# Attention read followed by a SiLU layer: the first w_in chunk in four transfers of 32 partitions, and three small early reads left out

## The chip, the cores and the metric

The kernel runs on one core of a Trainium2 chip. The core has five engines that run side by side, each with its own instruction queue: TensorE (PE, with its weight loads shown as PEld), VectorE (DVE), ScalarE (ACT), GpSimd (POOL) and SyncE (SP), which here only issues transfers. Transfers are carried out by 16 DMA engines that all queues share. The metric is the device time of one execution in microseconds (us), the median of several runs.

## The reference, cut to what matters

There are 8 batches of 8 heads, 512 positions of 64 numbers, and per head a state of 32 rows. Each position reads the state by attention, each state row reads the positions, and all 4352 rows, as vectors of 512, go through a layer with SiLU.

```python
scores = scale * np.matmul(x, state.transpose(0, 1, 3, 2))
a = softmax(scores)
xread = np.matmul(a, state)
scores2 = scale * np.matmul(state, x.transpose(0, 1, 3, 2))
sread = np.matmul(softmax(scores2), x)
x = concatenate([xread, sread], axis=2)   # then heads beside each other: 4352 x 512
h = x @ w_in                              # 512 x 2048
out = (h * (1.0 / (1.0 + np.exp(-h)))) @ w_out   # 2048 x 512
```

## The kernel before, in words

For the 512 position rows of a batch the kernel does not compute xread and multiply it by `w_in`; it computes W1 = state times `w_in` per batch (`w1_m`, L275, and `w1f_m`, L290, for the first chunk of batch 0), and then W1 times the transposed attention weights `aT` (`g1`, L313). W1 has four chunks of 512 columns. `g1(b, ft)` makes one of 16 blocks of 128 hidden columns, with SiLU on ScalarE into `g`; `g2` (L339) multiplies `g` by `w_out`. The sread rows of all batches go through `w_in` itself at the end (b = 8).

The order of every engine's instructions is written out by hand (`tc.manual_schedule`, L372): each engine runs its own in the order in which the Python code issues them, and waits on semaphores where data is not there. From L583 on a plan in steps of one `g2` matmul places the work of batches 2 to 7; before that, batch 0 and 1 are written out line by line.

What happens at the start:

- ScalarE's queue issues `st_f[0]` (L374, state of batch 0) and two of the three `tch` transfers (L375, L376); GpSimd issues the third (L383). A `tch` transfer reads 8 bytes from each eighth row of 128, 16 rows in four blocks, of `w_in` (columns 0 and 512) or `w_out`. Nothing uses what it brings.
- SP issues, in this order, the four quarters of x of batch 0 into `x_f` (L378, 256 KB each), `st_f[1]` (L379), the first 512 columns of `w_in` into `w_f` (L381, four transfers, one for each block of 128 rows of `w_in`, each over all 128 partitions) and the first quarter of `w_out` into `wo_f` (L437, four transfers). A DMA takes the next of eight semaphores in turn for the two hardware queues, so an issue can wait for the landing of the eighth one before it.
- TensorE runs filler matmuls on zeros (`warm`, L365) between the transposes of x (`x_T`, L140), the scores (`sc`, L172) and the transposes of state; VectorE and GpSimd cast x to bf16, ScalarE takes the exponential, VectorE and GpSimd normalise into `an` (L201, L213).
- After six fillers TensorE runs `w1f_m` (L478): W1 chunk 0 of batch 0 in float32 from `w_f` and `sbd_f`, eight matmuls of 64 rows by 32 columns of the array, for four blocks kt of `w_in` rows and two halves of 64 partitions; half 0 goes to bank w0 and half 1 to bank w1. The transposes of `an` (`a_T`, L223, matmuls at L229) stand behind them, then `g1(0, 0)` and `g1(0, 1)`.
- VectorE copies `aT`, a quarter of W1, casts `w_f` to bf16 into `w_in_sb` (L494 and L500, two blocks kt each; the copies themselves are recorded at L83), normalises sread (L257, L258) and casts `st_f[1]` (L496), whose transpose (L123) TensorE needs ahead of the first `g2`. GpSimd issues the loads of the other chunks (L101, L106) and of x of batch 1 (L95), and casts `wo_f` into `w_out_sb` (L475; recorded at L85).

Of the kernel before, what the change touches and what calls it, by code (L numbers as in the profile page):

```python
# [8 lines left out]
FP32 = mybir.dt.float32  # L9
# [10 lines left out]
def kernel(  # L20
# [8 lines left out]
    nc = tc.nc  # L29
    ds = bass.ds  # L30

    B, H, S, NS, D, DM, DF = 8, 8, 512, 32, 64, 512, 2048
    KT = 4
    SCALE = 0.125

    pers = ctx.enter_context(tc.tile_pool(name="pers", bufs=1))
# [3 lines left out]

    zeros = pers.tile([128, 512], BF16, name="zeros")
    ident = pers.tile([128, 128], BF16, name="ident")
    tch = [pers.tile([16, KT, 2], FP32, name=f"tch{i}") for i in range(3)]
    st_f = [pers.tile([128, 128], FP32, name=f"st_f{i}") for i in range(2)]
    w_f = pers.tile([128, KT, 512], FP32, name="w_f")
    wo_f = pers.tile([128, 4, DM], FP32, name="wo_f")
# [28 lines left out]
    win_re = moe_w_in.rearrange("(kt p) f -> p kt f", p=128)  # L75
    wout_re = moe_w_out.rearrange("(ft p) m -> p ft m", p=128)
# [211 lines left out]


    def w1f_m(bks):  # L290
        for kt in range(KT):
            for half in range(2):
                nc.tensor.matmul(  # L293
                    bank[bks[half]][ds(32 * kt, 32), :],
                    sbd_f[ds(64 * half, 64), kt, :],
                    w_f[ds(64 * half, 64), kt, :],
                    start=True,
                    stop=True,
                    skip_group_check=True,
                    tile_position=(64 * half, 32 * kt),  # L300
                )
# [70 lines left out]
    with tc.manual_schedule():  # L372

        nc.scalar.dma_start(st_f[0][:], state[0].rearrange("h ns d -> ns h d"))  # L374
        nc.scalar.dma_start(tch[0][:], win_re[0:128:8, :, 0:2])  # L375
        nc.scalar.dma_start(tch[1][:], wout_re[0:128:8, 0:4, 0:2])  # L376
        for kt in range(KT):
            load_x(0, nc.sync, kt, 1)  # L378
        nc.sync.dma_start(st_f[1][:], state[1].rearrange("h ns d -> ns h d"))  # L379
        for kt in range(KT):  # L380
            nc.sync.dma_start(w_f[:, kt, :], win_re[:, kt, 0:512])  # L381
        make_identity(nc, ident[:])
        nc.gpsimd.dma_start(tch[2][:], win_re[0:128:8, :, 512:514])  # L383
        nc.vector.memset(zeros[:], 0.0)
        nc.vector.memset(sbd[:], 0.0)
        for i in range(2):
# [89 lines left out]
        nc.scalar.preload_act_table(SILU)  # L476
        warm(6, "o0", 512)
        w1f_m(("w0", "w1"))  # L478
        w1_e(0, 0, ("w0", "w1"), ("act", "act"), 0, 256)
        a_T(0, (("a0", "dve"), ("a1", "dve")))  # L480
# [215 lines left out]
```

## Time and profile before

| what | value |
|---|---|
| median of 5 runs | 219.13 us (218.56 to 219.88) |
| the profiled execution | 219.13 us, its span 217.4 us |
| granted TensorE clock | 1.00 |
| DMA to landing, `x_f` by SP, 256 KB each | 3.9 us median |
| DMA to landing, `w_f` by SP, 256 KB each | 4.5 us median |
| DMA to landing, `wo_f` by SP, 256 KB each | 6.0 us median |
| DMA to landing, `tch`, 0.5 KB each | 3.6 to 3.7 us |

How to read the profile: its span runs from the first to the last instruction; the execution's own time is 1.7 us longer. L12 is line 12 of the kernel. A group of instructions is shown as line, engine, operation, output<-input and count, with the idle time of the engine ahead of it in brackets and what ended that. The chain that ended last is followed back from the last instruction: at each step to what released it, or to the instruction before it on its engine. Windows give, for a stretch of time, each engine's busy time and number of instructions, the clock, the mean busy share of the DMA engines (over 1 where an engine has several packets under way), and the GB/s written by them.

### The profile page before, as it was taken

What the parts mean: (1) busy time and instruction counts of PE and PEld (TensorE: products, weight loads), DVE (VectorE), ACT (ScalarE), POOL (GpSimd) and SP (SyncE); (2) the same over time, 40 slices, a digit from 0 to 9 for tenths busy, and PEclk for the clock granted to TensorE, in tenths of its full rate; (3) what the DMA queues carried; (4) which work ended last, traced back from release to release, by engine and by line L of the source; (5) the groups of instructions that cost most, each with busy time, mean ns of one, the idle gap of its engine ahead of it and who ended that gap; (6) DMA issues with size and microseconds to landing.
All of it is one profiled execution on the core that took longest, in us unless ns stands there. A gap on an engine that the chain in (4) does not pass through costs nothing.

```text
span 217.4 us, 4108 instructions
## 1 busy us (share of the span) xinstructions
PE 210.9 (97%) x1664; PEld 104.4 (48%) x1664; DVE 84.5 (39%) x176; ACT 134.3 (62%) x225; POOL 45.7 (21%) x87
## 2 busy tenths in 40 slices
PE   7989999999999999999999999999999999999993
PEld 7533454454444444444444444444454444566553
DVE  3775537832930463147313830275017401111110
ACT  3753485679767947884788458855885586233211
POOL 4696209300700070016001600070001000000000
PEclk9999999999999999999999999999999999999999
DMA  5999995695395149316831694146012311111112
GB/s 176 315 262 267 236 274 71 54 270 203 72 208 178 51 112 247 128 48 100 216 121 50 105 213 169 51 120 149 24 48 44 105 48 48 51 48 48 48 51 97
DMA packets 37555, 27.86 MB, mean 128 GB/s; under 512 B 22176, under 2 KB 31776, under 8 KB 37536
## 3 DMA queue, kind: packets, MB, share of 16 engines
q1 hardware_dynamic: 31280, 21.63, 37.3%
q0 software_dynamic: 5392, 5.44, 12.8%
q10 hardware_dynamic: 864, 0.53, 0.8%
q8 instruction: 13, 0.21, 0.4%
q14 instruction: 6, 0.05, 0.1%
HBM read 17.30 MB, written 8.91 MB: 121 GB/s over the span
## 4 chain that ended last, share of the span: by engine, by line
PE 94%; DVE 3%; ACT 1%; issue 0%; DVEq 0%; ACTq 0%
PE ps_o L342 28%; PE ps_w L342 26%; PE ps_h L318 25%; PE ps_h L329 3%; PE ps_o L367 2%; PE ps_a L175 2%; PE ps_a L278 1%; PE ps_w L293 1%; DVE w_in_sb L83 1%; PE ps_o L278 1%; PE ps_w L278 1%; PE ps_h L278 1%; DVE W L83 1%; PE ps_o L245 1%; DVE xT L83 1%; PE ps_a L143 0%
## 5 line engine op out<-in xcount | busy, mean ns | idle before, releaser
L326 ACT ACTIVATE g<-ps_h 128x512 bf16<-128x512 f32 x128 | 76.0, 597 | 36.4 <-PE ps_h L318 29.7
L318 PE MATMUL ps_h<-aT,W 128*128 128x512 bf16 x256 | 75.8, 379 | 0.2 <-DVE W L83 0.2
L342 PEld LDWEIGHTS <-g 128*128 128x128 bf16 x512 | 49.0, 98 | 54.9 <-issue 2.5
L342 PE MATMUL ps_w<-w_out_sb,g 128*128 128x512 bf16 x256 | 73.3, 379 | 0.0
L342 PE MATMUL ps_o<-w_out_sb,g 128*128 128x512 bf16 x256 | 65.9, 379 | 0.2
L318 PEld LDWEIGHTS <-W 128*128 128x128 bf16 x256 | 24.1, 98 | 27.8 <-DVE W L83 1.6
L201 POOL TENSOR_TENSOR an<-en,rs 128x512 bf16<-128x512 bf16 x8 | 8.4, 1054 | 111.9 <-ACT en L186 72.7
L83 DVE COPY o_sb<-ps_w 128x512 f32<-128x512 f32 (+1 forms) x13 | 8.5, 659 | 53.1 <-PE ps_w L342 53.0
L83 DVE COPY o_sb<-ps_o 128x512 f32<-128x512 f32 x14 | 9.5, 687 | 29.6 <-PE ps_o L342 29.5
L85 POOL CAST x_u<-x_f 128x256 bf16<-128x256 f32 x44 | 18.0, 453 | 0.0
L196 DVE TENSOR_REDUCE rs<-en 128x16 f32<-128x512 bf16 x14 | 9.2, 660 | 15.4 <-ACT en L186 15.3
L337 ACT ACTIVATE g_s<-ps_h 128x256 bf16<-128x256 f32 x16 | 6.1, 383 | 14.0 <-PE ps_h L329 14.0
L329 PE MATMUL ps_h<-xsT,w_in_sb 128*128 128x256 bf16 x64 | 9.6, 273 | 0.0
L83 DVE CAST W<-ps_a 128x512 bf16<-128x512 f32 x12 | 8.1, 683 | 3.7 <-PE ps_a L278 3.7
L87 ACT ACTIVATE o_sb<-ps_o 128x512 f32<-128x512 f32 (+1 forms) x4 | 2.2, 544 | 10.7 <-PE ps_o L342 7.9
L186 ACT ACTIVATE en<-ps_a 128x512 bf16<-128x512 f32 (+1 forms) x16 | 8.3, 568 | 0.5 <-PE ps_a L175 0.5
L329 PEld LDWEIGHTS <-w_in_sb 128*128 128x128 bf16 x64 | 6.3, 98 | 4.1
L186 ACT ACT_TABLE_LOAD x6 | 7.7, 1283 | 0.1
L609 ACT ACT_TABLE_LOAD x6 | 7.7, 1283 | 0.1
L87 ACT ACTIVATE o_sb<-ps_w 128x512 f32<-128x512 f32 (+1 forms) x5 | 2.7, 533 | 8.2 <-issue 6.6
L175 PEld LDWEIGHTS <-xT 128*128 128x128 bf16 x128 | 5.9, 98 | 3.8 <-DVE xT L83 0.8
L83 DVE CAST W<-ps_h 128x512 bf16<-128x512 f32 x9 | 6.1, 683 | 1.2 <-PE ps_h L278 1.2
(87 smaller groups left out, 169.0 us busy)
## 6 DMA issues: line engine op xcount, KB each, us to landing
out_dram<-o_sb SPq DMA_DIRECT2D x32, 256.0 KB, 2.7
x_f<-in_x_dram SPq DMA_DIRECT2D x5, 1024.0 KB, 6.8
w_in_sb<-in_moe_w_in_dram POOLq DMA_DIRECT2D x3, 512.0 KB, 9.7
w_out_sb<-in_moe_w_out_dram POOLq DMA_DIRECT2D x3, 512.0 KB, 10.1
x_f<-in_x_dram SPq DMA_DIRECT2D x4, 256.0 KB, 3.9
w_f<-in_moe_w_in_dram SPq DMA_DIRECT2D x4, 256.0 KB, 4.5
wo_f<-in_moe_w_out_dram SPq DMA_DIRECT2D x4, 256.0 KB, 6.0
x_f<-in_x_dram POOLq DMA_DIRECT2D x2, 512.0 KB, 9.5
```

The costliest lines, as they stand in the source:

```text
L83: nc.vector.tensor_copy(dst, src)
L85: nc.gpsimd.tensor_copy(dst, src)
L175: nc.tensor.matmul(v[:, kt % 2, :, c, :], xT[b % 2][:, kt, c, :], sbd[:, b, kt, :, :], start=True, stop=True, skip_group_check=True,)
L186: nc.scalar.activation(en[b % 2][:, :, :, ds(kt, n), :].rearrange("p h c k s -> p k (h c) s"), v[:, ds(kt % 2, n)], func=EXP, bias=0.0, sc ...
L196: nc.vector.tensor_reduce(v, en[b % 2][:, :, :, ds(kt, n), :], axis=AX, op=ADD)
L201: e.tensor_tensor(an[b % 2][:, ds(h0, hn), :, ds(kt, n), :].rearrange("p h c k s -> p (h c) k s"), en[b % 2][:, ds(h0, hn), :, ds(kt, n), ...
L278: nc.tensor.matmul(bank[bks[half]][ds(32 * kt, 32), :], sbd[ds(64 * half, 64), b, kt, half, :], w_in_sb[ds(64 * half, 64), kt, ds(512 * j, ...
L318: nc.tensor.matmul(bk[:], W1[b % 2][:, half, ds(128 * ft, 128)], aT[b % 2][:, half, :, :], start=(half == 0), stop=(half == 1), skip_group ...
L326: nc.scalar.activation(g[b % 2][:, ft, :], bk[:], func=SILU, bias=0.0)
L329: nc.tensor.matmul(bk[:, 0:256], w_in_sb[:, kt, ds(128 * ft, 128)], xsT[:, kt, :, :, :], start=(kt == 0), stop=(kt == KT - 1), skip_group_ ...
L342: nc.tensor.matmul(bank[bk][:, c0:c1], src[:, ft, ds(128 * tt, 128)], w_out_sb[:, ft, c0:c1], start=(ft == 0), stop=(ft == 15), skip_group ...
L609: nc.scalar.preload_act_table(SILU)
```

## The change

Four edits, all at the start of the program:

```diff
-    tch = [pers.tile([16, KT, 2], FP32, name=f"tch{i}") for i in range(3)]
...
     def w1f_m(bks):
-        for kt in range(KT):
-            for half in range(2):
+        for half in range(2):
+            for kt in range(KT):
                 nc.tensor.matmul(
...
         nc.scalar.dma_start(st_f[0][:], state[0].rearrange("h ns d -> ns h d"))
-        nc.scalar.dma_start(tch[0][:], win_re[0:128:8, :, 0:2])
-        nc.scalar.dma_start(tch[1][:], wout_re[0:128:8, 0:4, 0:2])
         for kt in range(KT):
             load_x(0, nc.sync, kt, 1)
         nc.sync.dma_start(st_f[1][:], state[1].rearrange("h ns d -> ns h d"))
-        for kt in range(KT):
-            nc.sync.dma_start(w_f[:, kt, :], win_re[:, kt, 0:512])
+        for i in range(4):
+            nc.sync.dma_start(w_f[ds(32 * i, 32)], win_re[ds(32 * i, 32), :, 0:512])
         make_identity(nc, ident[:])
-        nc.gpsimd.dma_start(tch[2][:], win_re[0:128:8, :, 512:514])
```

The three `tch` transfers and their tiles are gone. The four `w_f` transfers still carry 256 KB each, but each now fills 32 partitions with all four blocks kt, where each filled 128 partitions with one block. In `w1f_m` the four matmuls of half 0, which read partitions 0 to 63 and so the first two transfers, stand ahead of the four of half 1, which read the last two; before, each pair of matmuls needed one transfer. With three transfers fewer, the semaphores that the later transfers take, and wait for, move: by two places for those of SP and ScalarE, by one for those of GpSimd.

All other instructions keep their order on every engine. The short description that came with the change also speaks of W1 of chunk two a G2 group later; the two programs do not differ in that.

## The prediction

> **What bounds the kernel now.** I read the page first: the engines' totals and the chain that ended last.
>
> ```profile
> span 217.4 us, 4108 instructions
> PE 210.9 (97%) x1664; PEld 104.4 (48%) x1664; DVE 84.5 (39%) x176; ACT 134.3 (62%) x225; POOL 45.7 (21%) x87
> PE 94%; DVE 3%; ACT 1%; issue 0%; DVEq 0%; ACTq 0%
> ```
>
> TensorE is the bound: 210.9 of 217.4 us, and 94% of the chain is its own work. Part of that work is filler (L367), so the start has to be read by itself. The second view is the chain in order of time around the operations that the diff touches (start, length, what):
>
> ```profile
> 8.83 1.29 PE ps_o L367 x6
> 10.13 1.97 PE ps_w L293 x16
> 12.10 0.34 PE ps_a L229 x4
> ...
> 12.46 0.76 DVE aT L83 x2
> 13.22 0.33 DVE W L83
> 13.55 1.94 DVE w_in_sb L83 x2
> 15.49 0.09 DVE srec L257
> ...
> 15.89 0.16 DVE st_nat L83
> ...
> 16.10 0.23 PE ps_a L123
> ```
>
> Until 16.1 us the path goes from TensorE's first W1 (L293, `w1f_m`) through the transposes of `an` and a row of VectorE copies back to TensorE. The diff works on the input of L293. The third view, the timeline, and the waits of the first 20 us say what L293 waits for:
>
> ```profile
> 11.04 0.14 PEld L293 LDWEIGHTS ps_w<-w_f,sbd_f 64*32 64x32 f32 x4 [0.82 <-DMA w_f<-in_moe_w_in_dram]
> PE ps_a L123 <- DVE st_nat L83: 0.7, 1, 0.7
> ```
>
> Twelve of sixteen matmul records start at 10.06; the last four wait for the fourth `w_f` transfer until 11.04. At 16.10 TensorE stands still once more, 0.7 us for VectorE. The fourth view is the DMA load by windows (busy times in PE, PEld, DVE, ACT, POOL; clock; DMA share; GB/s) and the landing of `w_f`:
>
> ```profile
> 3.00:4.00 1.00, 1.00 (x12) 1.00 (x11) 0.29 (x1) 0.94 (x2) 0.29 (x1) 1.00 1.05 330
> 4.00:5.00 1.00, 1.00 (x12) 1.00 (x10) 0.19 (x1) 0.28 (x1) 0.38 (x2) 1.00 0.75 222
> 5.00:6.00 1.00, 1.00 (x12) 1.00 (x11) 0.29 (x2) 0.75 (x2) 0.36 (x1) 1.00 1.11 355
> 6.00:8.00 2.00, 1.77 (x30) 1.46 (x28) 1.39 (x5) 1.59 (x5) 1.58 (x3) 1.00 1.00 322
> 8.00:10.00 2.00, 1.80 (x15) 0.79 (x14) 1.92 (x7) 1.53 (x4) 0.96 (x2) 1.00 0.90 285
> 10.00:12.00 2.00, 2.00 (x17) 0.31 (x16) 0.63 (x1) 0.55 (x1) 2.00 (x4) 1.00 1.02 372
> DMA to landing us min/median/max: 4.2/4.5/5.5
> ```
>
> The 16 DMA engines are full from 3 us on, so `w_f` comes when the bytes ahead of it and its own have gone through. The last issue is at about 5.55 us, and 5.55 + 5.5 = 11.05 is the release at 11.04. Two windows stand out: 4 to 5 us, when the three `tch` transfers are under way (issued from 1.5 us, 3.6 to 3.7 us to landing), moves a third less; and 8 to 10 us, where `w_f` ends, moves 285 GB/s where the `wo_f` transfers right behind it, in rows of the same 2 KB, reach 372.
>
> **The change, part by part.** Everything is expressed as a shift of the last `w_f` landing (11.04 now), then carried to the end.
>
> *The three tch transfers go.* ScalarE loses issues of 0.61 and 0.45 us, but its next work on data starts at 3.97, when `st_f` (issued 0.74, 3.2 us to landing) is there: nothing gained. GpSimd loses 0.71 us and idles 1.5 us for `x_f` at that place anyway: nothing. On SP two waits for reused semaphores go, 0.4 us each ahead of a `w_f` issue; the engines are still full with `x_f` then (355 GB/s, share 1.11), which hides them; uncovered they would be worth 0.4. What can count is the window from 4 to 5: at the mean of its neighbours, 342 GB/s, it lost (342 - 222) / 342 = 0.35 us of moving. `x_f` also lands earlier, but the chain passes no wait for `x_f` after 6 us, so that alone is free. Ends 0 and -0.4 us, taken -0.3, since the dip lies where tch lies.
>
> What tch may have done for `w_f`, as a first reading of those rows, is lost. Its own trip is 3.7 us against 3.2 for `st_f`, so a cold start costs at most 0.5; but the first `x_f` transfer, which nothing reads ahead of, lands in 2.9 us, the shortest of all `x_f` transfers. Ends 0 and +0.5, taken 0.
>
> *Four transfers of 32 partitions.* Same 4 x 256 KB, same 2 KB rows, same number of issues. What changes is which rows the engines read together, and that all engines write into a quarter of the partitions. No transfer of this trace has that shape, so I bound it. `w_f` now moves through 6 to 10 us at (322 + 285) / 2 = 304 GB/s: 1.049 MB in 3.45 us. If the new rows cost no stalls it goes at the 372 of 10 to 12: 2.82 us, -0.63. On the reading side that is believable: the POOL chunk loads between 14 and 18 us, which also step through four row blocks per partition, write 206 GB/s in bf16, which is twice that in float32 read. If the engines get in each other's way in a quarter of the partitions so that two share what one had, it is 186 GB/s: 5.64 us, +2.19. No row is nearer to one end; I take the mean of the two times, 4.23 us: +0.78.
>
> [...]
>
> *The loop order in w1f_m.* Half 0 (transfers one and two) runs first, half 1 waits for three and four. Now four records follow the release and take 12.03 - 11.04 = 0.99 us until the transposes start; then eight would. Of the first twelve, six start within 0.03 us and the six second passes 0.45 later, so eight cost the same 0.99. Ends 0 and +0.45 (a second round), taken 0. Queued behind this wait on TensorE are the transposes of `an` (L229), and VectorE's aT copies wait for those. `an` itself is ready at 10.27 + 0.75 = 11.02, so nothing before about 11.05 can be gained.
>
> *Moved past the others.* `wo_f` stands behind `w_f` in the same queue and shifts with it. It lands from 6.02 + 5.7 = 11.7 on, and GpSimd casts it from 13.25: 1.5 us of cover. Beyond that GpSimd's casts and the loads issued after them would be late as well. The short description also names a W1 of chunk two that moves by a G2 group; the diff has no such edit and the order of the instructions after L293 is the same in both programs, so that costs nothing.
>
> *Sum.* -0.3 + 0 + 0.78 + 0 = +0.48 us for the landing and the transposes. After these VectorE works without a break from 12.46 to 17.9, TensorE follows at 16.10, and from 45 to 217 us TensorE is busy for 168.65 of 172 us: no slack takes the shift up. The profiled execution took 219.13 us (span 217.4, 1.7 around it), which is also the median of the five runs. 219.13 + 0.48 = **219.6 us**.
>
> **Rivals.**
>
> *Full rate, faster.* Both good ends: -0.35 - 0.63 = -0.98, landing at 10.06, transposes at the floor of 11.05. Then VectorE's first two `w_in_sb` casts start at 12.5 instead of 13.47, ahead of GpSimd's casts of `w_out_sb` (from 13.25, after three issues of 0.8 that start when `an` is done). Now those two casts take 2.03 us beside GpSimd; the later pair takes 0.94. The 1.09 saved removes the 0.7 us stop at 16.10, so up to -0.98 - 0.69 = -1.67: 217.5 to 218.2, middle 217.8. For it: the 285 GB/s window beside the 372. Against: the two windows of `w_f` together are only 0.63 us off the best.
>
> *Crowded partitions, slower.* One mechanism: sixteen engines writing into 32 partitions, at `w_f`, price up to +2.19 us less the 0.3 of tch. Slower begins where `w_f` takes 3.45 + 0.3 = 3.75 us, 280 GB/s, and passes 0.5% (1.1 us) at 4.85 us, 216 GB/s. Half rate gives 219.13 + 1.9 = 221.0; with no gain from tch 221.3. For it: each transfer's spread is what the diff shrinks. Against: no row of this trace shows the price.
>
> *The change does not do what it says.* The layout is neutral and the dip at 4 to 5 was not tch: 219.1, at best 218.8.
>
> **How the numbers follow.** Chances: forecast 0.40 (219.2 to 220.2), neutral 0.12, full rate 0.24, crowded 0.24 (220.2 to 221.3). The smallest difference that a measurement of this kernel tells from none is about 0.5%, 1.1 us: below 218.0 or above 220.2. Faster holds most of full rate, 0.22; slower holds crowded and the edge of the forecast, 0.28; the rest, 0.50, is within. The range goes from the far end of full rate, 217.5, to that of crowded, 221.2; a cold start of 0.5 us on top of the crowded end lies beyond it.
>
> **What would show it.** The wait of L293 for `w_f`: forecast near 11.5 us, full rate none or almost none, crowded 12.5 or later. The window from 4 to 5 us near 340 GB/s shows the tch term right; `w_f`'s windows at 372, near 250, or under 215 GB/s tell the three layouts apart. The start of L229 one microsecond after the release shows the loop order neutral. The stop ahead of L123 should stay 0.7 us in the forecast and vanish at full rate. The prediction is wrong if L293's wait moves and the start of L123 does not, or if times after 45 us change.

## The result, and the profile after

The changed kernel takes 220.79 us (median of 21 runs, 219.55 to 223.24); the kernel before, on the same chips, 219.31 us (40 runs, 218.56 to 220.41). The ratio is **1.0064, 95% interval 1.0047 to 1.0082**: 0.6% slower, 1.5 us by the medians. Two of the 21 executions, 222.98 and 223.24 us, lie over 1.5% above the fastest and are left out of the ratio, though all that the record shows of them is a lowered clock, as in six of those kept. Forecast was 219.6, with a range from 217.5 to 221.2.

The profiled execution of the changed kernel took 221.07 us, span 219.3 us (before: 219.13 and 217.4). On the page the totals and the clock slices say little by themselves:

```profile
span 219.3 us, 4109 instructions
PE 212.4 (97%) x1664; PEld 105.2 (48%) x1664; DVE 83.8 (38%) x176; ACT 134.4 (61%) x225; POOL 44.8 (20%) x86
...
PEclk9969999999999999999999999999999999999998
...
PE 89%; DMA 3%; SPq 2%; issue 2%; ACT 2%; DVE 1%; DVEq 0%; ACTq 0%
```

TensorE is busy for 1.5 us *longer* with the same 1664 matmuls, and the third slice of the clock (11 to 16.5 us) shows a 6 where all 40 slices of before had a 9: the same work at a lower clock. And 3% of the chain that ended last is now DMA, which was not in it before. The chain in order of time shows which one:

```profile
5.19 6.73 DMA w_f<-in_moe_w_in_dram
11.92 0.14 issue
12.05 1.06 PE ps_w L292 x8
13.12 0.96 PE ps_a L228 x8
```

The fourth `w_f` transfer lands at 11.92 us (11.00 before), `w1f_m` (now L292) goes on at 12.05 (11.04), the transposes of `an` (now L228) start at 13.05 (12.03). The timeline has the waits on TensorE, GpSimd and VectorE:

```profile
12.05 1.06 PE L292 MATMUL ps_w<-w_f,sbd_f 64*32 64x512 f32 x8 [0.88 <-DMA w_f<-in_moe_w_in_dram]
...
13.05 1.02 PE L228 MATMUL ps_a<-ident,an 128*128 128x128 bf16 x8
...
16.05 0.61 POOL L84 CAST w_out_sb<-wo_f 128x512 bf16<-128x512 f32 x1 [0.87 <-DMA wo_f<-in_moe_w_out_dram]
...
17.06 0.17 DVE L256 RECIPROCAL srec<-ps_a 128x2 f32<-128x2 f32 x1 [1.27 <-PE ps_a L244]
...
17.80 0.22 PE L122 MATMUL ps_a<-ident,st_nat 128*128 128x128 bf16 x1
```

The last line is the transpose that stood at 16.10 before: +1.70. The line above it is new: VectorE, which was the late one here, now waits 1.27 us for TensorE. The windows (columns as in the prediction) say why both are late:

```profile
4.00:5.00 1.00, 1.00 (x12) 0.98 (x10) 0.24 (x2) 0.24 (x1) 0.46 (x2) 1.00 1.02 330
...
6.00:8.00 2.00, 1.70 (x30) 1.46 (x28) 1.34 (x5) 1.54 (x5) 1.42 (x3) 1.00 1.08 235
8.00:10.00 2.00, 1.70 (x14) 0.79 (x14) 1.93 (x7) 1.53 (x4) 0.68 (x1) 1.00 1.06 228
10.00:12.00 2.00, 1.17 (x9) 0.15 (x8) 0.68 (x2) 0.99 (x2) 2.00 (x4) 1.00 1.05 257
12.00:14.00 2.00, 1.95 (x17) 1.14 (x18) 0.32 (x1) 0.66 (x2) 2.00 (x4) 0.77 1.11 319
14.00:18.00 4.00, 4.00 (x45) 1.43 (x44) 2.69 (x9) 1.63 (x3) 3.07 (x5) 0.69 1.23 214
```

From 6 to 10 us, where `w_f` moves, the DMA engines are as full as before (shares 1.08 and 1.06) and move 235 and 228 GB/s instead of 322 and 285. From 12 to 18 us the clock is 0.77 and 0.69 instead of 1.00; the trace's clock record has it halved from 13.09 to 16.51 us. The first line, 330 for 222, looks like the predicted end of the `tch` dip; the experiments will not bear that out.

Behind the start almost nothing happens: the 160 ScalarE activations at L325, taken one by one against those of before, are 1.69 us late from 28 to 88 us, and 1.86 at the last one.

### The profile page after: what moved, and what is told of

It is laid out like the page before. It is cut to its first block, busy times and chain, and to the rows that moved or that the text cites. A ratio compares the mean times of both kernels' runs of the same rounds, so it can differ in the third digit from the quotient of the medians.

```text
span 219.3 us, 4109 instructions
## 1 busy us (share of the span) xinstructions
PE 212.4 (97%) x1664; PEld 105.2 (48%) x1664; DVE 83.8 (38%) x176; ACT 134.4 (61%) x225; POOL 44.8 (20%) x86
## 4 chain that ended last, share of the span: by engine, by line
PE 89%; DMA 3%; SPq 2%; issue 2%; ACT 2%; DVE 1%; DVEq 0%; ACTq 0%
PE ps_o L341 27%; PE ps_h L317 26%; PE ps_w L341 25%; PE ps_h L328 3%; DMA w_f<-in_moe_w_in_dram 3%; PE ps_a L174 1%; PE ps_a L277 1%; SPq L94 1%; PE ps_w L277 1%; PE ps_o L277 1%; PE ps_h L277 1%; SPq L378 1%; PE ps_a L228 1%; DVE W L82 1%; ACT L605 1%
## 5 line engine op out<-in xcount | busy, mean ns | idle before, releaser
L325 ACT ACTIVATE g<-ps_h 128x512 bf16<-128x512 f32 x128 | 76.1, 597 | 38.1 <-PE ps_h L317 31.5
L317 PE MATMUL ps_h<-aT,W 128*128 128x512 bf16 x256 | 76.6, 383 | 0.2 <-DVE W L82 0.2
L174 PE MATMUL ps_a<-sbd,xT 128*128 128x64 bf16 x120 | 6.1, 193 | 0.8 <-DVE xT L82 0.8
```

The source lines that it names most:

```text
L174: nc.tensor.matmul(v[:, kt % 2, :, c, :], xT[b % 2][:, kt, c, :], sbd[:, b, kt, :, :], start=True, stop=True, skip_group_check=True,)
L317: nc.tensor.matmul(bk[:], W1[b % 2][:, half, ds(128 * ft, 128)], aT[b % 2][:, half, :, :], start=(half == 0), stop=(half == 1), skip_group ...
L325: nc.scalar.activation(g[b % 2][:, ft, :], bk[:], func=SILU, bias=0.0)
```

## The experiments

Lines of before (L293, L229, L123) are L292, L228, L122 in every kernel without the three `tch` tiles. "Narrow" below means that one transfer fills 32 neighbouring partitions.

**a_no_touch: the kernel before, without the three tch transfers.**

```diff
-        nc.scalar.dma_start(tch[0][:], win_re[0:128:8, :, 0:2])
-        nc.scalar.dma_start(tch[1][:], wout_re[0:128:8, 0:4, 0:2])
-        nc.gpsimd.dma_start(tch[2][:], win_re[0:128:8, :, 512:514])
```

> The kernel before with the three tch transfers left out and nothing else changed. Theory (the loss comes from w_f going into 32 partitions at a time, tch is a small burden): the window from 4 to 5 us moves about 330 GB/s and not 222, the last x_f quarter lands near 6.4 us and not 6.9, w_f keeps its rate near 300 GB/s, L293 is released 0.3 to 0.5 us earlier (near 10.6) and the time is 0.3 to 0.9 us below before. Rival (tch warmed the rows of w_in and w_out up, and the loss comes from its going): w_f lands at 11.5 us or later with 128 partitions as well, and the time is 0.5 us or more above before.

Measured: 218.99 us, ratio 0.9981 (0.9963 to 0.9999). Its windows:

```profile
4.00:5.00 1.00, 1.00 (x12) 1.00 (x10) 0.29 (x1) 0.20 (x1) 0.60 (x2) 1.00 0.93 318
...
6.00:8.00 2.00, 1.96 (x30) 1.69 (x28) 1.34 (x5) 1.54 (x5) 1.58 (x3) 1.00 0.74 180
8.00:10.00 2.00, 1.72 (x15) 0.80 (x14) 1.93 (x7) 1.53 (x4) 1.03 (x2) 1.00 0.93 305
```

The window from 4 to 5 us rises, but 6 to 8 falls from 322 to 180 at a share of only 0.74: single 2 KB packets of the first `w_f` transfer stand for up to 1.34 us (before: at most 0.80). The `w_f` issues come 0.36 us earlier, but the last landing is 10.92, only 0.08 us ahead of before's 11.00. The transpose L122 starts 0.50 us ahead of before's all the same, since VectorE's first two `w_in_sb` casts take 1.60 us here and not 2.03 (more on them under k). So the other part of the change, not this one, makes it slower.

**b_touch_kept: the change with the three transfers kept** (the new layout and loop order alone).

> The changed kernel with the three tch transfers put back: the new w_f transfers and the new loop order alone. Theory (32 partitions at a time): w_f moves at about 215 GB/s, the last one lands 0.3 to 0.5 us later than in the changed kernel, near 12.3 us, and the time is 0 to 0.5 us above the changed one (220.8 to 221.3). Rival (tch is what was missing): w_f moves at 300 GB/s or more, and the time falls to that of before or below.

Measured: 221.59 us, 1.0124 (1.0086 to 1.0163). In its trace the last `w_f` lands at 14.06 us and the clock is halved, here from 9.58 to 12.99, ahead of the wait's end. The layout alone costs what the change costs, and here 0.8 us more: all six executions have a lowered clock. The last quarter of `x_f`, ahead of `w_f` in the queue, lands at 8.90 us here (6.91 before, 6.42 in the changed kernel). Why the three reads should hurt beside the narrow transfers, where i below puts them near nothing and a at 0.4 us, is left open.

**c_spread32: the changed kernel, each transfer on every fourth partition.** Still 32 partitions, 32 rows in each of four blocks, 256 KB per transfer.

```diff
-            nc.sync.dma_start(w_f[ds(32 * i, 32)], win_re[ds(32 * i, 32), :, 0:512])
+            nc.sync.dma_start(w_f[i:128:4], win_re[i:128:4, :, 0:512])
```

> The changed kernel with each w_f transfer taking every fourth partition, so 32 partitions from 0 to 127 and not 32 neighbours; same bytes, same four blocks, same 32 rows to a transfer. Theory (neighbouring partitions share a narrow way in): w_f moves at 330 GB/s or more, the last one lands by 10.5 us, L228 starts at 11.1 to 11.5 us, and the time is 0.5 to 1.5 us below before (217.8 to 218.8). Rival (32 partitions are too few, whichever they are, or the four blocks 1 MB apart read badly): w_f stays near 215 GB/s, and the time is that of the changed kernel.

Measured: 219.11 us, 0.9989 (0.9973 to 1.0004): the whole loss is gone. Its windows of 6 to 10 us:

```profile
6.00:8.00 2.00, 1.64 (x26) 1.18 (x24) 1.39 (x5) 1.42 (x5) 1.62 (x3) 1.00 0.99 322
8.00:10.00 2.00, 1.88 (x14) 0.79 (x14) 1.90 (x7) 1.64 (x3) 1.19 (x2) 1.00 0.99 300
```

So it is not that a transfer has 32 partitions, but that they, or the rows read, lie side by side. The price of the spread is on SP: 0.60 us per issue instead of 0.43. The gain that was expected over before did not come (the last landing is 10.60, 0.40 earlier).

**e_rows_kept_spread and g_spread_rows_narrow** part the two sides that c changed together: e reads the rows of the changed kernel and writes them to every fourth partition; g reads every fourth row and writes to neighbouring partitions. In both the rows of the first chunk stand in the wrong places.

```diff
+            nc.sync.dma_start(w_f[i:128:4], win_re[ds(32 * i, 32), :, 0:512])     # e
+            nc.sync.dma_start(w_f[ds(32 * i, 32)], win_re[i:128:4, :, 0:512])     # g
```

> The changed kernel with the rows of each w_f transfer as they are, 32 neighbouring rows of w_in, but written into every fourth partition: the reading side of the change with the writing side spread. The rows of the first w_in chunk then stand in other partitions than the state that they are multiplied with, so the numbers of that chunk differ from the reference; the work and its order do not. Theory (32 neighbouring partitions take bytes in slowly): w_f moves at 300 GB/s or more in the 6 to 8 and 8 to 10 us windows, the last one lands near 10.5 us, no execution has a clock under 0.995, and the time is 218.5 to 219.3 us. Rival (rows 16 KB apart read slowly): windows near 230 GB/s, landing near 11.9 us, 220.8 us.

> The other corner: each w_f transfer reads every fourth of 128 rows and writes into 32 neighbouring partitions, so again the numbers of the first w_in chunk differ from the reference and the work does not. Theory (32 neighbouring partitions take bytes in slowly): windows 6 to 8 and 8 to 10 us near 230 GB/s, last landing near 11.9 us or later, time near 220.8 us (220.3 to 221.5). Rival (the rows decide): windows of 300 GB/s or more, landing near 10.5 us, time near 219.1 us.

(The rows of `w_in`, 2048 float32 numbers, are 8 KB apart, and not 16 as the expectation of e has it.) Measured: e 219.15 us, 0.9991 (0.9971 to 1.0012); g 220.54 us, 1.0056 (1.0032 to 1.0079). The windows of e, then of g:

```profile
6.00:8.00 2.00, 2.00 (x30) 1.88 (x28) 1.34 (x5) 1.54 (x5) 1.56 (x3) 1.00 0.95 321
8.00:10.00 2.00, 1.69 (x14) 0.79 (x14) 1.93 (x7) 1.53 (x4) 1.06 (x2) 1.00 0.93 279
```

```profile
6.00:8.00 2.00, 1.52 (x24) 1.32 (x22) 0.59 (x3) 1.54 (x5) 0.68 (x2) 1.00 1.09 235
8.00:10.00 2.00, 1.40 (x16) 0.94 (x18) 1.94 (x7) 0.85 (x3) 1.26 (x2) 1.00 1.06 233
```

g has the changed kernel's rate (235, 228) to within 3%, e that of c (322, 300) to within 7%. The rate goes with the partitions written, whichever rows are read. One of g's seven executions has a lowered clock, none of the twelve each of c and e.

**d_fillers: the changed kernel with eleven fillers ahead of w1f_m instead of six**, so that TensorE is busy through the longer wait.

```diff
-        warm(6, "o0", 512)
+        warm(11, "o0", 512)
```

> The changed kernel with 11 and not 6 filler matmuls of 512 columns ahead of w1f_m, which fill the 0.9 us in which TensorE waits for the second half of w_f. Theory (the loss has two parts, 1.0 us by the late landing and, in a part of the executions, about 0.7 us by a halved TensorE clock after the wait): the clock is 1.000 in all executions, the landing stays near 11.9 us, and the time is about 220.1, 0.3 to 0.8 us below the changed kernel. Rival (the halved clock does not come from the wait, or costs nothing): as many executions with a clock under 0.995 as in the changed kernel, 10 of 21, and the same time.

Measured: 220.09 us, 1.0051 (1.0025 to 1.0077); the clock is below 0.995 in 2 of 12 executions, both at 221.9 us. (For the changed kernel the expectation says 10 of 21; by the list of executions it is 8 of 21.) In the trace TensorE no longer waits ahead of L292. Fewer executions with a lowered clock than in the changed kernel is the direction that was expected, but the interval overlaps that of the change itself, so d alone decides nothing.

**f_order_only: a with the new loop order** (half 0, then half 1).

> The kernel before without tch and with the changed loop order in w1f_m, over the w_f transfers of before (one block of rows over all partitions each). Now half 0 as well needs all four transfers, so nothing of L292 starts until the last landing near 10.9 us. Theory (the order alone costs little): the sixteen records follow the landing in 1.0 us as four did, L228 starts near 12.0 us, and the time is that of a_no_touch, 218.8 to 219.4 us. Rival (the order is a part of the loss): halves one after the other take 1.5 us or more after the landing, L228 at 12.4 us or later, time 219.5 us or more, or the longer idle time halves the clock in some executions.

Measured: 219.37 us, 0.9998 (0.9981 to 1.0015), 0.4 above a. Against the expectation, six of the sixteen records of L292 start before the last landing. From the last landing to the start of L228 it is 1.05 us (11.20 to 12.25) in f and 1.03 us (10.92 to 11.95) in a: the order is worth nothing, the difference between the two traces is in the landing. f, like a, has the slow window from 6 to 8 us (172 GB/s).

**h_lighter_dve: a with a lighter VectorE between the two waits.** The second state tile is cast ahead of the `w_in_sb` casts, and the fourth of these goes to ScalarE.

```diff
+        cp("dve", st_nat[:, 1, :], st_f[1][:])
...
-        cp("dve", st_nat[:, 1, :], st_f[1][:])
...
-            cp("dve", w_in_sb[:, kt, 0:512], w_f[:, kt, :])
+        cp("dve", w_in_sb[:, 2, 0:512], w_f[:, 2, :])
+        cp("act", w_in_sb[:, 3, 0:512], w_f[:, 3, :])
```

> A version that should beat both: tch left out, w_f transfers and loop order as before, the cast of st_f[1] ahead of the w_in_sb casts on VectorE, and the fourth w_in_sb cast on ScalarE, which idles until 18.4 us. Theory (VectorE's row of copies from 12.4 to 17.6 us sets TensorE's pace there once w_f has landed): the stop ahead of L122 goes, the first W1 matmuls of batch 1 (L277) start about 0.5 us earlier than in a_no_touch (17.0 and not 17.5 us), and the time is about 218.5 us. Rival (another wait takes its place, or the landing of the second w_in chunk near 16.4 us): L277 at 17.5 us, and 219.0 us.

Measured: 218.86 us, 0.9972 (0.9959 to 0.9985), less than hoped, but faster than both kernels. In its trace L228 starts 0.32 us *later* than before and L122 0.53 *earlier*: there is slack between the two. That was the first plain sight of what the prediction had excluded.

**i_spread_touched: c with the three tch transfers; j_spread_lighter: c with h's VectorE edits and the old loop order.**

> The spread version (every fourth partition, c) with the three tch reads put back as they were, so that only tch differs from c. If tch itself costs what the prediction says (the dip from 4 to 5 us, 0.3 to 0.4 us of moving): the window from 4 to 5 us near 220 GB/s, the last w_f landing about 0.3 us later than c's 10.60, and 219.4 us. If the dip is a gap in the x_f transfers that comes and goes without tch as well (two executions without tch show 235 and 234 GB/s there), and tch costs nothing: 219.1 us. If the first reads of w_in rows are what tch pays for, this layout shows no slow window from 6 to 8 us with or without it, near 322 GB/s in both.

> The spread version with the two VectorE edits of h (the second state tile cast ahead of the w_in_sb casts, the fourth w_in_sb cast on ScalarE) and the loop order of before: the best parts together. If the gains add (c has its release 0.3 us ahead of a's, h is 0.13 us under a): 218.8 us. If the chain from the release to the first W1 of chunk two is bound elsewhere after the release (h released later than a and was still not slower): no better than h, 218.9, and no worse.

Measured: i 219.01 us, 0.9983 (0.9960 to 1.0006); j 218.89 us, 0.9976 (0.9956 to 0.9997). i is the fair test of `tch`, because c has neither the narrow transfers nor the slow window from 6 to 8 us: the last `w_f` landing is 10.60 us in both, and the times do not differ. Its window from 4 to 5 us shows 278 GB/s, so `tch` or not is not what that window measures: without `tch` it is 309 to 353 in a, c, d, e, f, l and the changed kernel, but 283, 267, 235 and 234 in j, k, g and h. What makes it swing stays open. j is no better than h: the gains do not add.

**k_after_again and l_after_third: the changed kernel unaltered, for two more traces.** Thirteen of the 21 executions had no lowered clock, and took 220.41 us in the median all the same; the one trace, with a release at 12.05 us (the start of L292 behind its wait for `w_f`), could not account for that.

> The changed kernel once more, unaltered, for a second trace of its start. So far one trace of it exists, with the release of L292 at 12.05 us and the TensorE clock halved from 13.09 to 16.51 us; yet 13 of 21 executions had no halved clock and still took 220.41 us in the median, 1.1 over before. The narrow versions' traces carry 0.8 us less to L122 than to L228 where the clock stays full (d: +0.58 and -0.18; g: +1.90 and +1.05). If that holds and the 1.1 us are all waiting, an execution without a halved clock has its release later than the traced one, near 13 us (L228 +1.9, L122 +1.1). If instead the release is near 12.05 in every execution and the 1.1 us come from somewhere behind the start: L228 +1.0, L122 near +0.2, and the shift grows after 20 us.

> The same kernel for a third trace, with the same two readings: if the waiting explains the time, the shift of L122 over before (16.10 us) equals the execution's time less 219.13 us within 0.3, whatever its release, and full clock takes 0.7 to 0.9 us off between L228 and L122 while a halved one adds there. If something behind the start costs the time, the two differ by more than 0.3 us.

Measured: k 220.26 us with a full clock, l 222.31 with a halved one. The timeline of k around the two waits:

```profile
12.80 1.06 PE L292 MATMUL ps_w<-w_f,sbd_f 64*32 64x512 f32 x8 [0.77 <-DMA w_f<-in_moe_w_in_dram]
...
13.80 0.62 PE L228 MATMUL ps_a<-ident,an 128*128 128x128 bf16 x8
...
15.24 1.19 DVE L82 CAST w_in_sb<-w_f 128x512 bf16<-128x512 f32 x2
...
17.03 0.23 PE L122 MATMUL ps_a<-ident,st_nat 128*128 128x128 bf16 x1
```

In before, VectorE's first pair of `w_in_sb` casts stands in the same view as

```profile
13.47 2.03 DVE L83 CAST w_in_sb<-w_f 128x512 bf16<-128x512 f32 x2
```

And l's clock by windows, beside its wait of 1.44 us:

```profile
12.00:14.00 2.00, 0.81 (x8) 0.18 (x8) 0.00 (x0) 0.20 (x1) 2.00 (x4) 0.90 1.04 342
14.00:18.00 4.00, 4.00 (x50) 1.85 (x46) 2.27 (x5) 1.32 (x4) 3.14 (x5) 0.62 1.22 216
```

The three traces of one and the same program, as shifts against before in us:

| trace | release of L292 (11.04 before) | L228 | clock | L122 | whole time, less 219.13 |
|---|---|---|---|---|---|
| after | 12.05 | +1.02 | halved from 13.09 | +1.70 | +1.94 |
| k_after_again | 12.80 | +1.77 | full | +0.93 | +1.13 |
| l_after_third | 13.19 | +2.67 | halved from 13.61 | +2.80 | +3.18 |

The first reading of k's expectation holds (release near 13, L122 +1.1). The execution's time follows L122 to within 0.2, 0.2 and 0.4 us; the last is outside the 0.3 that was asked, so some tenths are lost behind the start as well, 0.1 to 0.3 of them between 90 and 130 us. Traces without narrow transfers show such a drift too: it is 0 (i, j) to 0.3 (f) there, and 0.1 (b, d, k) to 0.65 (g) with them.

## Why the prediction was right or wrong

The time lies in the range, 1.2 us over the forecast, but in the band of the crowded rival (220.2 to 221.3, chance 0.24) and not in the forecast's own (219.2 to 220.2, chance 0.40). The mechanism named for the slower side is the right one; in the sum the main term is mis-sized, others are missing, and the step that carries the shift to the end is wrong.

- **The layout, +0.78: right mechanism, mis-sized.** The windows of 6 to 10 us hold 232, 232 and 235 GB/s in after, k and l, against 304 before, and the release came 1.0, 1.8 and 2.1 us late. At 232 GB/s the prediction's own sum takes 4.5 us for `w_f` and not 3.45, which is 1.1 us more; after's 1.0 is near that, k's and l's are not. The mean between "no stalls" and "half the rate" gave 248 GB/s, and the forecast's release near 11.5 was met in none of the three traces (after lies between the two); k and l lie in what the prediction kept for crowded partitions (12.5 or later). The windows, which count the bytes of other transfers too, show 225 to 245 GB/s for neighbouring partitions (after, d, g, k, l), where the old layout has 322 and 285 in before and every fourth partition 322 and 300 in c.
- **`x_f`, ahead of `w_f` in the queue: no term.** The prediction let it land earlier, at no price. Its last quarter lands at 6.91 us before, at 6.42 in after, 7.91 in k and 7.62 in l; from there to the last landing of `w_f` it is 4.1, 5.5, 4.8 and 5.4 us. So in k and l a part of the delay, 1.0 and 0.7 us, is there when `x_f` has landed. Why this landing swings by 1.5 us between executions of one program stays open.
- **"No slack takes the shift up": wrong, and it hid most of the mis-sizing.** The prediction took VectorE's row from 12.46 to 17.9 as solid work. It holds a collision. One `w_in_sb` cast of VectorE took 0.41 us by itself (at 15.96 us in before, at 15.38 in after); in before the first two took 0.72 and 1.39 beside GpSimd's casts of `w_out_sb`. When the transposes come later, the two engines meet in another phase (in k GpSimd's casts start 0.94 us later than in before, VectorE's 1.77): the pair takes 1.19 us in k instead of 2.03, and the stop of 0.7 us ahead of L123, which "should stay", shrinks to nothing on PE in that trace. At full clock the way from L228 to L122 is shorter than in before by 0.84 (k), 0.85 (g) and 0.76 (d), so of k's 1.77 us only 0.93 get through. In k the shorter pair makes the whole difference (2.03 - 1.19 = 0.84); in g and d the pair is 0.97 and 0.85 shorter, a tenth more than the way. The prediction had this saving in its full-rate rival, where an *earlier* start was to bring it; a later one brings it too.
- **A term that is missing: the TensorE clock.** In the traces of after and l the longer wait of L292 was followed by a halved clock for 3.41 us. The mean clock of the two executions was 0.989 and 0.992; 8 of the 21 executions have a mean of 0.989 to 0.992, and the others, with the 83 of the kernel before that the experiments list, 0.997 or more. That the wait brings it on is argued, not shown: e and j wait 1.06 and 0.99 us at the same place, and none of their 24 executions has a lowered clock. The halved clock falls on the transposes, `g1` and the state's path (13.09 to 16.51 us in after), VectorE waits for TensorE at L256 (1.27 us in after), and the saving above turns into a loss. If the saving of 0.85 is taken off the shift of the release (1.01 and 2.15), after is left with +0.16 and l with +1.30; they measured +1.70 and +2.80: by this estimate **1.5 us for each halved clock**. That agrees with the executions' medians, 222.1 with and 220.41 without a lowered clock, 1.7 apart. Together the two groups give the median: most executions like k (+1.1), over a third with 1.5 to 1.7 more.
- **The tch term, -0.3: not a fixed price.** The dip from 4 to 5 us, from which it was read, comes and goes without `tch`; it was one window of one trace. What leaving `tch` out gains depends on the layout: nothing in the spread one (c against i), 0.4 us in the old one (a against before, 0.02 to 0.8 by the interval; but the landing is only 0.08 us ahead there), 0.8 us beside the narrow transfers (the change against b), for reasons that no run shows. Removing the waits on SP did move the issues 0.36 us forward, as read from the trace.
- **The cold start, 0: wrong in the old layout, right in the new.** Without `tch` the old layout shows 180, 172 and 165 GB/s from 6 to 8 us (a, f, h) where before has 322, and its last landings, 10.92, 11.20 and 11.32, are 0.1 earlier to 0.3 later than before's in spite of the earlier issue; so, if the earlier issue counts in full, the slow window costs 0.3 to 0.7, around the upper end of 0.5. The rows of the changed kernel, written without crowding (c, e, j), show 316 to 322, though they too have single packets of 1.3 to 1.9 us, a little later (7 to 10 us); a long packet alone does not make the window slow. Whether `tch` or another difference spares before these stalls was tried only by taking it out. The first `x_f` transfer's short trip was no evidence for another tensor.
- **The loop order, 0: right.** L228 starts 1.0 us after the release in after and k, 0.99 in before.
- **wo_f behind: right that it costs nothing.** Its 1.5 us of cover are used up (GpSimd's fourth cast waits 0.87 us in after, 0.84 in l), but nobody waits for that cast at this place.
- **After 45 us nothing changes: right** to within 0.1 to 0.3 us.

So that the time fell into the range is in part luck. 219.6 came near it by errors of opposite sign: release too early by 0.5 to 1.7 us and no clock term on the one hand, 0.85 of slack not seen on the other. Of the rivals, crowded partitions named what happened; full rate is excluded by the windows, and "layout neutral" by c, e and g.

The narrow transfers are the fault of this change. Of the versions run, h (the old layout without `tch`, a lighter VectorE) has the lowest ratio, 0.9972 of before, with j and a (0.9976, 0.9981) inside its interval; and c (0.9989) shows that 32-partition transfers lost nothing when the partitions were spread.

## What to carry to other kernels

When a transfer is cut into pieces, look at which partitions each piece fills: here every fourth partition in place of a block of neighbours cost 0.17 us more per issue and gave the whole rate back (322 and 300 GB/s in c, 235 and 228 in the changed kernel). VectorE's row of work beside GpSimd's was not of a fixed length here: look whether single instructions of the same shape have different lengths in such a row (0.41 to 1.39 us in before) before calling it free of slack. And look at the clock behind a longer wait of TensorE: in the traces of after and l a halved clock followed the wait, an estimated 1.5 us more; that the wait brings it on is not shown.

## What the runs showed of the hardware

- With four transfers of 256 KB into blocks of 32 neighbouring partitions the windows from 6 to 10 us show 225 to 245 GB/s (after, d, g, k, l; 179 and 211 in b), with the DMA engines full (1.02 to 1.09); into every fourth partition 279 to 322 (c, e, i, j). By the trace's packet records a 2 KB packet took 139 to 164 ns there in the changed kernel (88 to 115 before), in means over 1 us, and the 4-byte packets that ran among them 13 to 18 ns instead of 9: what shared the engines with these transfers was slower too.
- With a strided set of partitions SP took 0.60 us for each `w_f` issue (c, e, i, j); the narrow `w_f` transfers took 0.43 in the changed kernel but for the first, which took 0.59.
- The entries of the clock record, up to the last, are 3.41 us long or a multiple of it: 211.63 us at full clock in before (62 times), 6.83 full, 3.41 halved and 201.39 full in after (2, 1 and 59 times). In the piece of 3.41 us ahead of a halved one TensorE was busy for 0.74 (after), 0.58 (l) and 0.39 (b) of the time, but pieces of 0.66 to 0.71 (k, g, j) were not followed by a halved one, nor those of 0.76 to 0.78 with the waits of c, e and i. The share by itself does not decide, and what does stays open.
- A VectorE cast of 128x512 from float32 to bf16 took 0.41 us alone (before, after) and up to 1.39 beside GpSimd casts of the same shape, which took 0.60 to 0.85 (before).
